# The opening of an mLSTM and MoE kernel in another order and smaller pieces, with its large tiles at multiples of 256 bytes

## The chip, the cores and the metric

The kernel runs on one core of one Trainium2 chip. The time is the device time of one execution in microseconds (us); lower is better. A core has five engines that run their own instruction streams and wait for each other by semaphores: TensorE (PE; its weight loads are listed as PEld), VectorE (DVE), ScalarE (ACT), GpSimd (POOL) and SyncE (SP), which here only issues transfers. Matmuls take their operands from SBUF and write PSUM, whose eight banks are handed out as tiles.

## The reference

Three stages, all in float32:

- An mLSTM over 2 sequences of 768 steps with 8 heads of 40: per step a running maximum m of the gates, a matrix memory C and a vector n with decay exp(f + m_old - m) and input weight exp(i - m), and the output y = sigmoid(o) * (C q) / max(|n q|, 1).
- A mixture of four experts on the 1536 tokens of 320 features: out = sum over e of p_e * relu(x w1[e]) w2[e], with 1024 hidden features and p the normalised domain_probs.
- A gated layer: ((x w_a) * (x w_b)) w_out, with 1536 hidden features.

## The kernel before

**Precision.** A float32 operand that goes through fast matmuls (type fp32r) is kept as a high part and the rest, `wh` and `wl` for weights, `xh` and `xl` for x, `hh` and `hl` for hidden values, and a product adds up three terms. High parts come from a cast, low parts from a subtraction.

**Weights.** There are 14 blocks (8 of the experts, 6 of the gated layer). A block of the experts is 2816 columns, loaded in eight pieces of 352 (`piece1`). It is a generator of three steps: issue the load of the raw piece; cast it to `wh` on ACT; subtract to `wl` on POOL or DVE, as the table LOENG says. Raw pieces of blocks 0 to 2 lie in the space of `acc`, the sums that are not yet in use; a piece whose place is still in use makes its load wait, and SP with it. Blocks lie in three places: pool `wp0` (0, 1, 2, 4, 5, 6, 9, 10, 11), `wp1` (3, 7, 12) and `wx` (8, 13). By the sizes of the tiles allocated ahead of them the tiles of `wp0`, x (`xp`) and h (`hp`, `hp2`) start 160 bytes over a multiple of 256, those of `wp1` 224 and those of `wx` 96; all offsets inside a tile are multiples of 256.

**Tokens.** They go in 12 tiles n of 128, two tiles (one of each sequence) to a chunk j. A tile passes: gates (`gate1`, `gate_d`, `gate2`, `gate_c`, then hi and low parts into `zh`, `zx` and `LT`, and `build_R`, which spreads L over the heads into `Rr`); decay weights (`mask_of`, `weights_of` on PE, `w_exp` on ACT, `w_mask` on POOL; only the chunks 0 and 1 do it this way); scores q k (`scores2` or `scores`, tile `pt_c`); their product `s1b` on DVE; `s2a` on PE (`pt_y`, and from chunk 1 on `pt_i` with the state); `s2b` and `s2x` on DVE, which give x (`x_t`); three transposes `s3a`, then `x_hi` on ACT and `x_lo` on DVE. The state of a sequence moves on by `weigh_k`, `state` (`pt_u`), `state_in`, `state_old`, `state_add`.

**Order.** Scheduling is manual: each engine runs its instructions in the order in which the program emits them. The list `ev` (from L701) holds pairs of a slot number and a call, is sorted by slot, and is emitted between the items of the first stage. An item k is one hidden block of 128 features for 256 tokens: a first product of eight matmuls (L209, into `psa`), its eviction by ACT (`hh`, L276) and DVE (`hl`, L277), and two items later the second product of six matmuls (L288 to L290). Slots under 0 come ahead of item 0; there are 12 items for each pair of tiles, so item 12 needs x of the tiles 2 and 3. Two tiles of `psa` and two of `psb` take turns, and four PSUM tiles `ps_t` serve the attention work. Matmuls of a dummy operand (`warm_up`, `pt_w`) fill gaps of PE.

**Later.** From block 3 on the weights meet 512 tokens at a time, in `quad_a` (L229: 60 matmuls of 512 columns, two at once in two halves of the rows; weights are the loaded operand, x streams) and `quad_b` (L254: h is loaded, weights stream).

What the change touches: `piece1` (L75 on) and its table of places; `warm_up` (L641 on); `mask_of` (L481 on); `s2x` (L562 on) with its third multiply L577; `s2c` (L626 on); the list from L701 to about slot 12; and the pools' sizes.

Of the kernel before, what the change touches and what calls it, by code (L numbers as in the profile page):

```python
# [33 lines left out]
LOENG = {0: "ppvppppp", 1: "pppvpppv", 2: "ppppvvvp", 3: "vpvpvpvp", 4: "vpvpvpvp", 5: "vpvpvpvp"}  # L34
# [15 lines left out]
def mlstm_moe_kernel(ctx, tc, gates, qk, qc, kvo, dp, w1b, w2b, ident_d, bdmask_d, rsel_d, exp_d, out):  # L50
# [24 lines left out]
    def piece1(i, s, pool, lo_eng, apart=False, dma=None):  # L75
# [231 lines left out]
    with ExitStack() as c1:  # L307
# [9 lines left out]
        G = 112  # L317
        bdmask = ac.tile([120, 3, 3 * DE], F32, name="bdmask")
# [243 lines left out]
        def s2x(n):  # L562
# [10 lines left out]
            if j == 0:  # L573
# [3 lines left out]
                nc.vector.tensor_tensor(x[:, DM:], xu.rearrange("p h d -> p (h d)")[:, 256:DM], og[j][:, b, 256:DM], op=ALU.mult)  # L577
# [48 lines left out]
        def s2c(n):  # L626
            x = td[n]["x"]
            nc.scalar.copy(x[:, DM:], x[:, 256:DM])
# [12 lines left out]
        def warm_up(n):  # L641

            for _ in range(n):
                nc.tensor.matmul(pw, wz[:, 0:P], wz, start=True, stop=True)
# [14 lines left out]
        w0, w1, w2 = ([piece1(i, f, wp0, nc.vector if LOENG[i][f] == "v" else nc.gpsimd) for f in range(NP1)] for i in range(3))  # L659
# [340 lines left out]
```

## Time and profile before

| what | us |
|---|---|
| median of 3 runs | 611.43 |
| lowest, highest | 611.16, 614.92 |
| the profiled execution | 613.7 |
| its span, first to last instruction | 612.0 |
| PE busy in the span | 599.4 |
| DVE, ACT, POOL busy | 406.4, 274.6, 189.3 |

The profile is of one execution. Its span leaves out what lies around the first and last instruction. Busy is the time in which an engine has at least one instruction running; since matmuls overlap, a PE that is busy all the time may still run them further apart than it could. PE's granted clock has two levels, 1.2 and 2.4 GHz; the profile gives the share of the full one.

### The profile page before, as it was taken

To read this page: it belongs to the slowest core of one execution; us is meant where nothing else is said; L and a number is where in the kernel's file an instruction comes from. 1 tells how busy PE (TensorE), PEld (TensorE's weight loads), DVE (VectorE), ACT (ScalarE), POOL (GpSimd) and SP (SyncE) were. 2 spreads that over 40 slices of the span, in tenths; PEclk is the share of its full clock that TensorE was granted. 3 is DMA by queue.
4 is the path that set the end of the run, shared out by engine and by line. 5 is a ranking of instruction groups with operands and counts; after the bars stand their busy time and mean duration, and the time that the engine had idled before them with its cause. 6 is when DMAs were issued, how large, how long until landed. Compare 5 with 4: busy or idle time off the path is not lost.

```text
span 612.0 us, 14366 instructions
## 1 busy us (share of the span) xinstructions
PE 599.4 (98%) x5815; PEld 564.3 (92%) x5816; DVE 406.4 (66%) x820; ACT 274.6 (45%) x633; POOL 189.3 (31%) x225
## 2 busy tenths in 40 slices
PE   8789999999999999999999999999999999999997
PEld 5689999999999899999999999988898989888886
DVE  6978767676553243323789899898777787864344
ACT  7737566666533323333344343454553434341211
POOL 2756516363511111334243333333222222310000
PEclk9989999999999999999999999999999999999999
DMA  8956473738202122322222222222121120200012
GB/s 246 251 172 168 134 203 90 212 81 221 59 13 69 36 60 74 82 73 76 57 76 59 72 71 60 57 64 65 47 49 45 37 56 22 69 4 2 2 44 87
DMA packets 29344, 51.51 MB, mean 84 GB/s; under 512 B 3509, under 2 KB 18141, under 8 KB 29277
## 3 DMA queue, kind: packets, MB, share of 16 engines
q1 hardware_dynamic: 15869, 26.06, 15.5%
q10 hardware_dynamic: 12496, 22.16, 13.4%
q0 software_dynamic: 912, 2.36, 1.3%
q8 instruction: 46, 0.75, 0.5%
q14 instruction: 21, 0.17, 0.1%
HBM read 47.79 MB, written 2.00 MB: 81 GB/s over the span
## 4 chain that ended last, share of the span: by engine, by line
PE 93%; DVE 4%; DMA 1%; issue 0%; ACT 0%; SPq 0%; DVEq 0%; ACTq 0%
PE psy L254 27%; PE psa L229 27%; PE psb L229 11%; PE psa L209 10%; PE psy L288 3%; PE pt_y L539 3%; PE psy L290 3%; PE psy L289 3%; PE pt_i L545 1%; PE pt_c L525 1%; PE pt_u L601 1%; DMA qk_t<-in_qk 1%; DVE Rr L478 1%; PE pt_x L146 0%; DVE qs_t L353 0%
## 5 line engine op out<-in xcount | busy, mean ns | idle before, releaser
L229 PE MATMUL psa<-xh,wh 64*128 64x512 f32 x576 | 135.2, 390 | 0.0
L254 PE MATMUL psy<-wl,hh 64*128 64x320 f32 x752 | 131.4, 305 | 0.0
L254 PE MATMUL psy<-wh,hh 64*128 64x320 f32 x752 | 131.3, 305 | 0.0
L254 PE MATMUL psy<-wh,hl 64*128 64x320 f32 x752 | 131.2, 305 | 0.0
L229 PE MATMUL psa<-xh,wl 64*128 64x512 f32 x414 | 97.4, 389 | 0.0
L254 PEld LDWEIGHTS psy<-wh,hh 64*128 64x128 f32 x752 | 85.7, 184 | 0.8
L229 PEld LDWEIGHTS psa<-xh,wh 64*128 64x128 f32 x576 | 80.9, 184 | 5.9 <-issue 0.9
L254 PEld LDWEIGHTS psy<-wl,hh 64*128 64x128 f32 x752 | 85.5, 184 | 0.8
L254 PEld LDWEIGHTS psy<-wh,hl 64*128 64x128 f32 x752 | 85.7, 184 | 0.0
L229 PE MATMUL psa<-xl,wh 64*128 64x512 f32 x384 | 85.6, 389 | 0.0
L849 DVE SCALAR_TENSOR_TENSOR hl<-psa,hh 128x512 fp32r<-128x512 f32 x60 | 38.6, 685 | 54.8 <-ACT hh L848 54.4
L126 POOL TENSOR_TENSOR wl<-tp,lf 128x272 fp32r<-128x272 f32 x48 | 39.1, 814 | 113.0 <-DVE tp L125 111.3
L229 PE MATMUL psb<-xh,wh 64*128 64x512 f32 x216 | 69.8, 389 | 0.0
L229 PEld LDWEIGHTS psa<-xh,wl 64*128 64x128 f32 x414 | 60.7, 184 | 3.7
L229 PE MATMUL psb<-xh,wl 64*128 64x512 f32 x180 | 58.5, 389 | 0.0
L229 PEld LDWEIGHTS psa<-xl,wh 64*128 64x128 f32 x384 | 55.2, 184 | 3.6
L277 DVE SCALAR_TENSOR_TENSOR hl<-psa,hh 128x256 fp32r<-128x256 f32 x72 | 30.4, 422 | 41.4 <-ACT hh L276 40.9
L123 POOL TENSOR_TENSOR lf<-lf,sq 128x272 f32<-128x272 f32 x48 | 38.1, 795 | 62.6 <-ACT wh L122 48.7
L94 POOL TENSOR_TENSOR wl<-raw,wh 128x352 fp32r<-128x352 f32 x28 | 26.4, 948 | 95.1 <-ACT wh L92 68.7
L276 ACT ACTIVATE hh<-psa 128x256 fp32r<-128x256 f32 x72 | 27.6, 384 | 60.5 <-PE psa L209 59.7
L848 ACT ACTIVATE hh<-psa 128x512 fp32r<-128x512 f32 x60 | 32.6, 596 | 46.7 <-PE psy L254 26.9
L209 PE MATMUL psa<-xh,wh 128*128 128x256 f32 x216 | 51.6, 293 | 1.3 <-DVE hl L277 1.0
(146 smaller groups left out, 1424.5 us busy)
## 6 DMA issues: line engine op xcount, KB each, us to landing
raw<-in_w2b ACTq DMA_DIRECT2D x48, 272.0 KB, 2.8
qk_t<-in_qk SPq DMA_DIRECT2D x16, 480.0 KB, 5.5
raw<-in_w1b ACTq DMA_DIRECT2D x32, 176.0 KB, 2.3
acc<-in_w1b SPq DMA_DIRECT2D x24, 176.0 KB, 3.9
kvo_t<-in_kvo SPq DMA_DIRECT2D x10, 364.5 KB, 5.9
Rr<-dL_t ACTq DMA_DIRECT2D x5, 512.0 KB, 4.5
og_t<-in_kvo SPq DMA_DIRECT2D x6, 320.0 KB, 5.0
out<-acc SPq DMA_DIRECT2D x12, 160.0 KB, 1.9
```

The source lines that it names most:

```text
L94: lo_eng.tensor_tensor(wl[:, cs], raw, wh[:, cs].bitcast(F32), op=ALU.subtract)
L123: nc.gpsimd.tensor_tensor(lf, lf, sq, op=ALU.mult)
L126: nc.gpsimd.tensor_tensor(wl[:, cs], tf, lf, op=ALU.add)
L209: nc.tensor.matmul(ps, l, r, start=(i == 0), stop=(i == len(prs) - 1))
L229: return nc.tensor.matmul(ps[g], w[rows, o:o + P], x, start=start, stop=stop)
L254: ms = [nc.tensor.matmul(ps[t], l[rows, t * P:(t + 1) * P], w[rows, off:off + DM], start=start, stop=stop) for t, rows in zip(two, (UP, DN))]
L276: nc.scalar.activation(self.hh, ps, AF.Relu)
L277: nc.vector.scalar_tensor_tensor(self.hl, ps, 0.0, self.hh.bitcast(F32), op0=ALU.max, op1=ALU.subtract)
L288: nc.tensor.matmul(ps, lh, wh[:, off:off + DM], start=(fi == 0), stop=False)
L289: nc.tensor.matmul(ps, lh, wl[:, off:off + DM], start=False, stop=False)
L848: nc.scalar.activation(hh, ps[f], AF.Relu)
L849: nc.vector.scalar_tensor_tensor(hl, ps[f], 0.0, hh.bitcast(F32), op0=ALU.max, op1=ALU.subtract)
```

## The change

- **Pieces.** The places of raw pieces come from a table LAND; the third and fourth piece of block 1 use the rotating raw tiles instead of places in `acc`. The casts of the first two pieces of block 0 move from ACT to POOL, and all of block 0's subtractions are on POOL (one was on DVE). Subtractions that POOL does for blocks 0 to 2 are split into two halves of 176 columns.
- **x.** In chunk 0 the third multiply (the 64 columns that are kept twice) is replaced by a copy on POOL (`s2c`); the copies of tiles 2 and 3 move from ACT to POOL.
- **First loads.** The gates and two of the four first q/k loads go from SP's queue to ACT's, the other two and `rsel` from ACT's to SP's. Later loads come in another order.
- **Opening.** The four masks come together, the scores of tile 1 behind the weights of tile 0; hi and low parts of the gates are made on DVE; the first chunk's `build_R` uses DVE and ACT, not POOL; there are fewer fillers.
- **Second chunk.** Gates, weights, scores, states and the pieces of blocks 1 and 2 get other slots between 0 and 12.
- **Addresses.** `dpt` and `psm` move into the space of the last `acc` tile; small tiles `even`, `side` and `brim` are added that nothing reads or writes. With them `wp0`, `wp1`, `wx`, x and h start at multiples of 256.

```diff
-LOENG = {0: "ppvppppp", 1: "pppvpppv", 2: "ppppvvvp", 3: "vpvpvpvp", 4: "vpvpvpvp", 5: "vpvpvpvp"}
+LOENG = {0: "pppppppp", 1: "pppvpppv", 2: "ppppvvvp", 3: "vpvpvpvp", 4: "vpvpvpvp", 5: "vpvpvpvp"}
+LAND = ((0, 1, 2, 3, 4, 5, 6, 7), (8, 9, None, None, 0, 1, 2, 3), (4, 5, 6, 7, 8, 9, 2, 3))
...
-    dpt = const.tile([P, NT, E], F32, name="dpt")
     pg = const.tile([P, NT, E], F32, name="pg")
-    psm = const.tile([P, NT, 1], F32, name="psm")
+    even = const.tile([P, 24], F32, name="even")
+    side = ctx.enter_context(tc.tile_pool(name="side", bufs=1, side="right")).tile([P, 56], F32, name="side")
...
-        if i < 3:
-            at = (s if i == 0 else 8 + s if s < 2 else s) * st
-            raw = sums[:, at:at + st]
+        at = LAND[i][s] if i < 3 else None
+        if at is not None:
+            raw = sums[:, at * st:(at + 1) * st]
...
-        nc.scalar.copy(wh[:, cs], raw)
+        copy_on(hi_eng, wh[:, cs], raw)
         yield
-        lo_eng.tensor_tensor(wl[:, cs], raw, wh[:, cs].bitcast(F32), op=ALU.subtract)
+        parts = 2 if i < 3 and lo_eng is nc.gpsimd else 1
+        for k in range(parts):
+            ps = slice(s * st + k * st // parts, s * st + (k + 1) * st // parts)
+            lo_eng.tensor_tensor(wl[:, ps], raw[:, k * st // parts:(k + 1) * st // parts], wh[:, ps].bitcast(F32), op=ALU.subtract)
...
-                nc.vector.tensor_tensor(x[:, DM:], xu.rearrange("p h d -> p (h d)")[:, 256:DM], og[j][:, b, 256:DM], op=ALU.mult)
...
-        def s2c(n):
+        def s2c(n, eng=nc.scalar):
             x = td[n]["x"]
-            nc.scalar.copy(x[:, DM:], x[:, 256:DM])
+            copy_on(eng, x[:, DM:], x[:, 256:DM])
...
-            (-40, load_gates, 0, nc.sync), (-39.9, load_rsel, nc.scalar), (-39.8, load_qk, 0, 0, nc.sync), (-39.7, load_qk, 0, 1, nc.scalar),
+            (-40, load_gates, 0, A_), (-39.9, load_rsel, nc.sync), (-39.8, load_qk, 0, 0, A_), (-39.7, load_qk, 0, 1, nc.sync),
...
-            (-35, mask_of, 0, 0, ps_b, "b"), (-34.95, mask_of, 0, 1, ps_b, "b"), (-34.93, mask_of, 1, 0, ps_a, "a"), (-34.9, scores2, 0), (-34.85, warm_up, 1), (-34.83, scores2, 1),
-            (-34.81, warm_up, 0), (-34.8, gate1, 0), (-34.7, gate_d, 0, V), (-34.5, gate2, 0), (-34.4, gate_c, 0), (-34.3, hi_L, 0, nc.scalar),
-            (-34.2, hi_cm, 0, nc.gpsimd), (-34.15, top_cm, 0, nc.scalar), (-34.1, low_L, 0), (-33.9, low_cm, 0, nc.gpsimd),
-            (-33.8, build_R, 0, V, 0, 4), (-33.7, build_R, 1, nc.gpsimd, 0, 4), (-33.6, build_R, 0, nc.scalar, 4, 8), (-33.5, build_R, 1, V, 4, 8),
-            (-33, weights_of, 0, 0), (-32.9, w_exp, 0, 0), (-32.7, weights_of, 0, 1),
+            (-35, mask_of, 0, 0, ps_b, "b"), (-34.95, mask_of, 0, 1, ps_b, "b"), (-34.93, mask_of, 1, 0, ps_a, "a"), (-34.92, mask_of, 1, 1),
+            (-34.9, scores2, 0),
+            (-34.8, gate1, 0), (-34.7, gate_d, 0, V), (-34.5, gate2, 0), (-34.4, hi_L, 0, V), (-34.3, low_L, 0),
+            (-34.2, build_R, 0, V, 0, 4), (-34.15, gate_c, 0), (-34.1, hi_cm, 0, V), (-34.05, low_cm, 0), (-34, build_R, 0, A_, 4, 8),
+            (-33.9, build_R, 1, V, 0, 4), (-33.8, build_R, 1, A_, 4, 8),
+            (-33, weights_of, 0, 0), (-32.9, w_exp, 0, 0), (-32.7, weights_of, 0, 1), (-32.6, w_exp, 0, 1),
+            (-32.5, scores2, 1), (-32.4, weights_of, 1, 0), (-32.3, w_exp, 1, 0), (-32.1, weights_of, 1, 1), (-32, w_exp, 1, 1),
...
-            (-28.9, go, w0[4:5]), (-28.88, go, w0[5:6]), (-28.87, gate1, 1), (-28.86, gate_d, 1, V), ...
+            ... (-28.5, gate1, 1), (0.2, gate_d, 1, V), (0.3, gate2, 1), ...
...
-            ... (3.871, weights_of, 2, 0), ... (5.343, scores2, 3), ... (5.45, state, 1), ... (5.523, load_kvo, 3), ...
-            ... (5.6, s2a, 2, 1), ... (5.9, weights_of, 3, 0), ... (7.379, s2a, 3, 0), ...
+            ... (2.3, build_R, 2, V, 0, 4), ... (3.25, build_R, 2, V, 4, 8), ... (4.7, weights_of, 2, 0), ... (5.74, load_kvo, 3),
+            ... (5.8, weights_of, 3, 0), ... (6.5, weights, ), ... (6.7, scores2, 3), ... (6.88, send_L, 2, nc.sync), ... (6.91, state, 0), ...
+            ... (7.1, s2a, 2, 1), ... (7.45, spread_L, 4, nc.sync), ... (7.6, s2a, 3, 0), ... (8.12, state, 1), ...
...
+    brim = ctx.enter_context(tc.tile_pool(name="brim", bufs=1, reuse_waits="tile")).tile([P, 16], F32, name="brim")
```

## Rows read from the trace of the kernel before

**Rows 1.** The profile page: busy us by engine (share of the span, instructions).
```profile
PE 599.4 (98%) x5815; PEld 564.3 (92%) x5816; DVE 406.4 (66%) x820; ACT 274.6 (45%) x633; POOL 189.3 (31%) x225
```

**Rows 2.** Stretches: busy us (x instructions) of PE, PEld, DVE, ACT, POOL; clock; DMA share, GB/s.
```profile
18.90:59.00 40.10, 35.33 (x256) 33.01 (x257) 33.69 (x66) 25.88 (x62) 27.09 (x28) 0.96 0.69 193
59.00:75.00 16.00, 15.24 (x123) 15.01 (x123) 12.39 (x25) 10.35 (x30) 7.64 (x11) 1.00 0.43 112
...
25.00:30.00 5.00, 3.70 (x23) 2.86 (x23) 4.87 (x8) 4.74 (x14) 3.90 (x6) 1.00 0.68 201
30.00:35.00 5.00, 4.17 (x38) 3.74 (x37) 4.97 (x8) 3.06 (x9) 5.00 (x6) 1.00 0.42 109
35.00:40.00 5.00, 4.26 (x23) 4.19 (x22) 3.27 (x8) 0.48 (x1) 1.03 (x1) 0.66 0.36 102
```

**Rows 3.** Opening by time: start, length, engine, line; in brackets the wait before.
```profile
7.98 1.16 PE L517 MATMUL pt_c<-qk_t 40*128 40x128 f32 x16
...
9.07 0.98 PE L494 MATMUL pt_a<-Rr,LT 112*128 112x512 f32 x3
...
14.32 3.01 POOL L94 TENSOR_TENSOR wl<-acc,wh 128x352 fp32r<-128x352 f32 x3 [5.90 <-DMA qk_t<-in_qk]
14.68 0.96 DVE L577 TENSOR_TENSOR x_t<-xu_t,og_t 128x64 f32<-128x64 f32 x1
...
17.61 0.21 DVE L577 TENSOR_TENSOR x_t<-xu_t,og_t 128x64 f32<-128x64 f32 x1
...
18.92 0.50 PE L209 MATMUL psa<-xh,wh 128*128 128x256 f32 x2 [0.35 <-ACT xh L134]
```

**Rows 4.** Chain of the first items and just after: start, length, what.
```profile
52.79 0.63 PE pt_u L601 x6
...
59.14 0.96 PE psa L209 x8
...
71.55 0.85 PE pt_y L539 x8
72.41 0.70 PE pt_i L545 x6
```

**Rows 5.** PE's waits from 0 to 75 us: total, times, longest.
```profile
PE psa L209 <- DVE hl L277: 1.0, 2, 0.8
PE pt_a L494 <- DVE Rr L478: 0.9, 1, 0.9
PE pt_c L517 <- DVE w_t L529: 0.8, 1, 0.8
...
PE pt_u L601 <- DVE cbd_t L609: 0.7, 1, 0.7
```

**Rows 6.** DVE, POOL and ACT by time, columns as in rows 3.
```profile
4.60 0.29 DVE L393 TENSOR_TENSOR df<-fa,gt 112x128 f32<-112x128 f32 x1
...
6.62 2.35 DVE L478 TENSOR_TENSOR Rr<-zx,rsel 64x512 fp32r<-64x512 f32 x2
...
19.33 3.81 POOL L94 TENSOR_TENSOR wl<-acc,wh 128x352 fp32r<-128x352 f32 x4 [1.99 <-ACT wh L92]
...
20.59 0.86 DVE L393 TENSOR_TENSOR df<-fa,gt 112x128 f32<-112x128 f32 x1
...
44.87 0.24 ACT L628 COPY x_t<-x_t 128x64 f32<-128x64 f32 x1
```

**Rows 7.** Chain of the row-paired stage: start, length, what.
```profile
311.02 6.83 PE psa L229 x60
...
366.46 7.00 PE psa L229 x60
...
579.84 3.51 PE psy L254 x48
...
590.24 3.52 PE psy L254 x48
```

**Rows 8.** DMA issues of the first 40 us: KB each, median us to landing.
```profile
kvo_t<-in_kvo SPq DMA_DIRECT2D x3, 364.5 KB, 6.5
```

More of the change, by code (lines that the diff above doesn't have):

```diff
@@ L73, in mlstm_moe_kernel, with copy_on, piece1 @@
     wblk = {}
-    def piece1(i, s, pool, lo_eng, apart=False, dma=None):
+    def copy_on(eng, o, i):
+        (eng.copy if eng is nc.scalar else eng.tensor_copy)(o, i)
+    def piece1(i, s, pool, lo_eng, apart=False, dma=None, hi_eng=nc.scalar):
         if s == 0:
@@ L317, in mlstm_moe_kernel @@
         G = 112
+        dpt = sums[:, 3776:3824].rearrange("p (n e) -> p n e", e=E)
+        psm = sums[:, 3824:3836].unsqueeze(2)
         bdmask = ac.tile([120, 3, 3 * DE], F32, name="bdmask")
@@ L639, in mlstm_moe_kernel, with warm_up @@
         nc.gpsimd.memset(wz, 0.0)
-        def warm_up(n):
+        def warm_up(n, ps=None):
+            if ps is None:
+                ps = ps_b.tile([P, 512], F32, tag="b", name="pt_w")
             for _ in range(n):
-                nc.tensor.matmul(pw, wz[:, 0:P], wz, start=True, stop=True)
+                nc.tensor.matmul(ps, wz[:, 0:P], wz, start=True, stop=True)
         def go(gens):
@@ L657, in weights @@
             nc.vector.tensor_tensor(pg, dpt, psm.to_broadcast([P, NT, E]), op=ALU.mult)
-        w0, w1, w2 = ([piece1(i, f, wp0, nc.vector if LOENG[i][f] == "v" else nc.gpsimd) for f in range(NP1)] for i in range(3))
+        w0, w1, w2 = ([piece1(i, f, wp0, nc.vector if LOENG[i][f] == "v" else nc.gpsimd, hi_eng=nc.gpsimd if i == 0 and f < 2 else nc.scalar) for f in range(NP1)] for i in range(3))
         V = nc.vector
@@ new lines, in mlstm_moe_kernel @@
+            (1.5, go, w1[1:2]), (2.2, go, w1[2:3]), (2.21, go, w1[3:4]), (2.25, hi_cm, 1, V), (2.26, low_cm, 1), (2.3, build_R, 2, V, 0, 4),
+            (2.4, go, w1[2:3]), (3.1, go, w1[3:4]), (3.15, go, w1[4:5]), (3.2, go, w1[5:6]), (3.25, build_R, 2, V, 4, 8),
+            (3.3, gate4, 0), (3.31, gate5, 0), (3.4, go, w1[4:5]), (3.6, build_R, 3, V, 0, 4), (4.1, go, w1[6:7]), (4.15, go, w1[7:8]),
+            (4.4, gate_tail, 0), (4.45, gate_out, 0),
+            (4.7, weights_of, 2, 0), (4.71, w_exp, 2, 0), (4.72, w_mask, 2, 0), (4.73, go, w1[5:6]), (4.8, build_R, 3, V, 4, 8), (4.9, s1b, 2, 0),
@@ new lines, in mlstm_moe_kernel @@
+            (5.1, gate4, 1), (5.11, gate5, 1),
+            (5.3, weights_of, 2, 1), (5.31, w_exp, 2, 1), (5.32, w_mask, 2, 1), (5.4, go, w1[6:7]), (5.5, s1b, 2, 1), (5.6, go, w1[7:8]),
+            (5.7, go, w2[4:5]), (5.71, go, w2[5:6]), (5.72, go, w2[6:7]), (5.73, go, w2[7:8]), (5.74, load_kvo, 3),
+            (5.8, weights_of, 3, 0), (5.81, w_exp, 3, 0), (5.82, w_mask, 3, 0), (5.85, weigh_k, 0),
+            (6.1, go, w2[0:1]), (6.2, go, w2[1:2]), (6.3, s2a, 2, 0),
+            (6.5, weights, ), (6.52, gate1, 2), (6.53, gate_d, 2, V), (6.55, weights_of, 3, 1), (6.56, w_exp, 3, 1), (6.57, w_mask, 3, 1), (6.6, gate_tail, 1), (6.62, gate_out, 1), (6.64, table, AF.Sigmoid), (6.65, o_gate, 2),
@@ new lines, in mlstm_moe_kernel @@
+            (6.7, scores2, 3), (6.75, go, w2[0:1]), (6.8, go, w2[1:2]), (6.85, s1b, 3, 0), (6.87, gate2, 2), (6.88, send_L, 2, nc.sync), (6.94, gate_c, 2),
+            (6.9, state_old, 0), (6.91, state, 0), (6.92, state_in, 0), (6.93, state_add, 0), (7.1, s2a, 2, 1), (7.15, go, w2[2:3]), (7.16, go, w2[3:4]), (7.18, table, AF.Exp), (7.2, s2b, 2), (7.25, s2x, 2), (7.3, s2c, 2, P_), (7.35, s1b, 3, 1),
+            (6.98, weigh_k, 1), (7.45, spread_L, 4, nc.sync), (7.55, spread_L, 5, nc.sync), (7.4, go, w2[2:3]), (7.5, go, w2[3:4]), (7.6, s2a, 3, 0),
@@ new lines, in mlstm_moe_kernel @@
+            (8.1, state_old, 1), (8.12, state, 1), (8.13, state_in, 1), (8.14, state_add, 1), (8.15, go, w2[4:5]), (8.16, go, w2[5:6]),
+            (8.2, s3a, 2), (8.25, x_hi, 2), (8.3, x_lo, 2), (8.4, go, w2[4:5]), (8.45, go, w2[5:6]), (8.5, s2a, 3, 1), (8.6, s2b, 3), (8.65, s2x, 3), (8.7, s2c, 3, P_),
+             (7.95, weigh_k, 2), (8.8, go, w2[6:7]), (8.9, go, w2[6:7]),
+            (9.1, go, w2[7:8]), (9.3, go, w2[7:8]),
+            (9.65, weigh_k, 3),
+            (8.0, load_qk, 4, 0), (8.02, load_kvo, 4), (9.75, load_gates, 3), (8.03, load_qk, 4, 1),
```

71 lines of the change are left out of this document (27 added, 44 removed).

## The prediction

> **What bounds it now.** I read the page's busy times, then the stretches, then the opening in order of time, then the chain and TensorE's waits. TensorE (PE) is busy for 98% of the span [rows 1], so time can only come from three places: the opening before the first product of the experts, the waits behind it, and the length of a matmul itself. The stretches place the waits: from 59 to 75 us PE is busy for 15.2 of 16.0, before that it is idle or slow again and again [rows 2]. The first product starts at 18.92, released by the cast of xh [rows 3]; the thirteenth item, near which the touched order ends, starts at about 59.0 (59.14 where the chain cuts it) [rows 4]. That stretch is 40.1 us. PE's work in it, from rows where it runs without a wait [rows 3, 4]: 12 first products at 0.96 (11.5), 10 second products of six matmuls at 0.147 (8.8; a pair of the same 320 columns takes 3.51/24 in [rows 7]), four s2a at 0.85 (3.4), two pt_i at 0.70 (1.4), four states at 0.63 (2.5), one scores2 at 1.16 and four weight matmuls of 0.3 or less (2.2), and 1.0 for the transposes, an estimate from their columns. That is 30.8, so 9.3 us are lost there. Of them 3.4 are the four longest waits [rows 5] and 1.7 the clock: 0.66 of it granted over the 5 us from 35 on, so partly the lower level of 1.2 GHz, after the waits of 0.8 and 0.7 [rows 2, 5]. The rest is short waits and the refill of PE after each. In the same stretch VectorE (DVE) is busy for 33.7 of 40.1, and at 97% (4.87 of 5) from 25 to 30 [rows 2]: it is DVE that PE waits for.
>
> **Term a, up to the first product.** Now the scores of the second tile start at 7.98, the weight matmuls behind them at 9.07, x of the second tile is done at 17.82 (17.61 and 0.21) [rows 3]. The new order puts the weight matmuls of tile 0 ahead of the scores of tile 1. They then wait for the gates, since low_cm goes from GpSimd (POOL) to DVE, behind the first build_R. The first of two builds begins at 6.62, 2.35 for both [rows 6]; with cm moved behind it, it begins near 6.35 and ends near 7.5, and three small instructions of about 0.3 (the subtract's 0.29 [rows 6]) make LT ready near 8.5, some 0.5 before 9.07. From there PE is bound by the 32 pt_y matmuls, which wait for the same DVE products as now; I take 0.25 of the 0.5. On x, the third multiply of each tile goes: 0.96, about 0.9 of it behind the one before, and 0.21 [rows 3]. In its place stands a copy of 64 columns on POOL. ScalarE (ACT) does that copy in 0.24 [rows 6]; for POOL no row has it, and I take 0.4 for the one that counts, the second (0.24 below, 0.95 above, where a piece of wl stands ahead of it). 0.25 + 1.1 - 0.4 is about 0.9; the wl piece that ran on DVE leaves the queue ahead of the low part of x, for which I add 0.3. **a = 1.2**, between 0 and 2.0. Costed at nothing: the casts of the first two pieces of w0 go from ACT to POOL, which stood idle for 5.9 us up to 14.32 [rows 3] and has done them before x. The first loads trade places between SP and ACT, three issues on each ahead of the scores as before; ACT's table load starts some 0.3 later and is covered by the wait for zx, and without that cover the 0.3 would be paid once.
>
> **Term b, from the first product to the thirteenth.** What each wait is now and what the change does to it [rows 5, 6]. The 0.8 for hl: DVE does the scan and the subtract of the second pair (the latter 0.86) ahead of the first eviction; the subtract moves behind it. The 0.9 for Rr: weights_of(2) goes from slot 3.87 to 4.7, its builds end a slot before. The 0.8 of scores2(3), for a bank that s1b must free, moves from slot 5.3 to 6.7, and the 0.7 of the state products from 5.45 to 8.12. Loads: w1's first pieces get places of their own, so SP waits less for pieces of w0 to be used up, with qk, kvo and gates behind it; the spread of L goes from ACT to SP. Against that, DVE's own work stays: it adds hi_L (about 0.3) and moves nothing off after the first product. So DVE sets the bound: 33.7 us at the 97% that it has reached are 34.7, and 0.7 I leave for evictions that it cannot begin before PE's product ends: 35.4 against 40.1. **b = 4.6** with the hi_L. The ends are 0 (DVE idles as often as now) and 9.3 (its instructions shrink beside shorter ones of POOL, and PE never waits). Late next: POOL makes the low pieces of w0 at 0.95 each (3.81 for four [rows 6]) behind the second copy of x, so that items 2 and 3 may wait some 0.3 each, and in slots 3 and 8 DVE has four to six long instructions ahead of an eviction. Both are within what is left of the 9.3.
>
> The subtract took 0.86 beside POOL's pieces and 0.29 ahead of them [rows 6]. The Trainium skill, SBUF — State Buffer, section "SBUF: two separate sides", says that VectorE with two SBUF inputs and GpSimd take a port pair in turn, and that the first holds it for its whole instruction; the trace agrees with these 0.86. By that rule pieces of half the length would shorten a block by 0.24 on average, at some ten meetings 2.4 us (an estimate from that page), and the sum would be 10.0 in place of 7.6; by the same rule the copies that POOL takes over from ACT block DVE, which speaks against the change. The sum takes neither; shorter instructions on DVE are priced from rows as a rival below.
>
> **Term c, the addresses.** The sizes of the tiles put wp0 (blocks 0 to 2, 4 to 6, 9 to 11), x and h at 160 bytes over a multiple of 256, wp1 (3, 7, 12) at 224 and wx (8, 13) at 96. The row-paired stage differs in step with that: the 60 matmuls of quad_a take 6.83 with wp0 and 7.00 with wp1, and with wx a second product of 3.51 begins 10.40 before the next, which leaves 6.89 [rows 7]. The second products keep their 3.5 with wx and, by the chain, elsewhere, and in them the weights stream and h is loaded; so it is the loaded operand that matters. If multiples of 256 run like wp0, the nine units of wp1 save 0.17 each (1.5) and the six of wx 0.06 or less (0.3). **c = 1.8.** No row has these tiles at 0. The other end is that 0 is as bad as 224: the 24 quads that are not in wp1 pay 0.17 (4.1), and the 576 first products' matmuls of the 72 items the same 5.8 ns (3.3), together 7.4. More gain than 2.0 is left out: 6.83/30 is 14 ns over 512 columns at 2.4 GHz and 3.51/24 is 13 ns over 320, alike for two sizes and two places, so that rest looks like a fixed step. I take 1.8, since wp0 is the level of most rows and the distance from weights to x, 0 in wp0, is 0 everywhere afterwards.
>
> The 550 us behind the thirteenth item are otherwise not touched; dpt and psm, now in the space of the last acc tile, are read at slot 6.5, long before that tile is written.
>
> **Sum.** 1.2 + 4.6 + 1.8 = 7.6. The profiled execution took 613.7 (612.0 of span and 1.7 around it); one like it would take 606.1. It stands 2.3 over the median of the runs, 611.43, from which the forecast is 603.8, said as 604.
>
> **Rivals.** *The waits only change place.* load_kvo(3) is issued at slot 5.74, but its buffer is that of tile 0, free when state(0) has run at 6.91, and s2a(3) needs it at 7.6. Between them PE has a first and a second product, half an s2a with pt_i: about 3.4 us. A kvo load took 6.5 from issue to landing in the first 40 us [rows 8]: PE would wait some 3 us, and the clock could fall as at 35 us (1.7). Behind the waiting load SP holds send_L(2), both spreads of L and the loads of tile 4, all for slot 12 and later. For it: on PE state(0) stands behind scores2(3) and weights_of(3), which need banks that DVE and ACT free; against: the DMA share was 0.42 after 30 us and 0.68 before [rows 2]. 603.8 + 4.6 is 608.4, which is also b = 0. 22 in 100. *The addresses have nothing to do with it*, the 0.17 belongs to what runs beside: c = 0, 605.6. 12 in 100. *Full closing*: b near 8, as DVE's instructions get short without POOL's long pieces: 600.4. 16 in 100. *The clock falls in the opening*: the single fillers between scores, weights and pt_y go, and PE waits about 1 us before the weights. After waits of 0.8 and 0.7 the clock fell once [rows 2, 5]; at its lower level the 32 pt_y would take 4 times 0.85, 3.4 us, more [rows 4]: 607.2. 8 in 100. The Trainium skill, TensorE: Matmul & The Clock Gate, section "HAM oscillation — how this bites in real kernels", warns of idle stretches between bursts of matmuls; the trace agrees at 35 us. *Slower*: multiples of 256 cost what 224 costs, in every quad and item: 7.4 against a gain of 5.8 from a and b, 613.0. It decides from 7.00 per quad on. For it stands only that nothing lies there now, against it wp0. 7 in 100.
>
> **Numbers.** The forecast itself, 601 to 606.5, has 35 in 100. A measurement of this kernel can tell about 1%, 6.1 us: faster is under 605.3, slower over 617.5. Faster: 0.25 of the forecast's own, 0.16 of full closing, 0.09 of the address case and the others: 0.50. Slower: 0.05, the slower rival with less than a and b gained. Same: 0.45. The range goes from full closing with c and a at their best to the moved waits with half of a: 598 to 610.
>
> **What would show it.** The first product near 17.7; the thirteenth item 35 to 36 us later; PE's waits for hl, Rr and cbd gone and the clock at 1.00 from 35 to 40; quads of blocks 3, 7 and 12 at 6.83. Wrong if a wait for kvo_t or a low clock stands before 45 us, if DVE's work in the stretch grows, or if quads with wp0 leave 6.83.

## The result, and the profile after

| | before | after |
|---|---|---|
| median, us (4 runs each) | 611.90 | 605.81 |
| lowest to highest | 611.16 to 614.92 | 605.27 to 606.00 |
| the profiled execution | 613.7 | 606.0 |
| its span | 612.0 | 604.3 |

The 611.90 has one run more than the 611.43 from which the forecast was taken. The ratio is 0.989, with an interval from 0.9855 to 0.9924: 6 us less. The forecast of 604.0 was 1.8 too low. A first account comes from four stretches of the two traces:

| stretch | before | after | difference | predicted |
|---|---|---|---|---|
| first product of item 0 starts | 18.92 | 17.19 | -1.7 | -1.2 (a) |
| from there to the thirteenth item | 40.05 | 35.48 | -4.6 | -4.6 (b) |
| from there to the row-paired stage | 145.14 | 145.51 | +0.4 | 0 |
| first quad_a to the start of the last second product of a block | 396.37 | 394.49 | -1.9 | -1.8 (c) |
| sum | | | -7.8 | -7.6 |

The profiled executions differ by 7.7 us, just as the sum said, yet the medians differ by 6.1. Where the other 1.6 us went is answered behind the experiments, in the first point on the prediction.

The page after, busy times, against [rows 1]: PE has lost 5.6 us of busy time while its number of instructions stayed (two fewer on the page). So part of the gain is work that got shorter, not waits that went.

```profile
PE 593.8 (98%) x5813; PEld 561.1 (93%) x5814; DVE 403.5 (67%) x821; ACT 273.3 (45%) x630; POOL 193.0 (32%) x248
```

The stretches after (columns as in [rows 2]; line numbers of the changed kernel are 5 to 9 higher from here on):

```profile
17.20:52.70 35.50, 33.33 (x256) 31.42 (x257) 31.35 (x68) 25.45 (x59) 27.68 (x45) 1.00 0.82 232
...
25.00:30.00 5.00, 4.93 (x35) 4.52 (x33) 4.73 (x9) 3.93 (x10) 5.00 (x7) 1.00 1.08 292
30.00:35.00 5.00, 4.90 (x44) 4.37 (x43) 4.50 (x10) 3.88 (x9) 5.00 (x9) 1.00 0.39 126
35.00:40.00 5.00, 3.82 (x32) 3.67 (x32) 4.34 (x11) 2.62 (x5) 1.62 (x3) 1.00 0.46 141
```

PE's busy share from the first product to the thirteenth item rises from 88% to 94%, the clock from 35 to 40 is 1.00 where it was 0.66, and DVE's work is 31.35 us, not 33.69. The largest hole left lies in the 5 us from 35 on; a second, of 0.6, stands at 47.9. PE's waits from 0 to 75 us (total, times, longest), against [rows 5], say which ones:

```profile
...
PE pt_i L551 <- DVE cbd_t L614: 1.2, 1, 1.2
PE pt_a L500 <- DVE LT L443: 1.2, 1, 1.2
PE pt_c L531 <- DVE qs_t L362: 0.9, 1, 0.9
PE pt_x L153 <- DVE x_t L585: 0.6, 1, 0.6
PE psa L216 <- ACT xh L141: 0.4, 1, 0.4
...
```

All four long waits of [rows 5] behind the first product are gone: hl, Rr, the bank of w_t, and cbd ahead of pt_u. A new one for cbd, longer than the old (1.18 against 0.7), stands elsewhere, ahead of pt_i at 37.4. The opening by time, against [rows 3] and [rows 6]:

```profile
6.41 0.68 DVE L484 TENSOR_TENSOR Rr<-zx,rsel 64x512 fp32r<-64x512 f32 x1
...
8.19 0.70 PE L500 MATMUL pt_a<-Rr,LT 112*128 112x512 f32 x2 [1.16 <-DVE LT L443]
...
8.82 1.16 PE L523 MATMUL pt_c<-qk_t 40*128 40x128 f32 x16
...
15.94 0.24 POOL L77 COPY x_t<-x_t 128x64 f32<-128x64 f32 x1 [0.41 <-DVE x_t L582]
...
17.19 0.51 PE L216 MATMUL psa<-xh,wh 128*128 128x256 f32 x2 [0.35 <-ACT xh L141]
...
19.28 0.29 DVE L402 TENSOR_TENSOR df<-fa,gt 112x128 f32<-112x128 f32 x1
```

The first weights start at 8.19 (9.07 before), after a wait for LT; the scores of tile 1 come behind them. One build_R took 0.68 where two took 2.35 beside POOL's [rows 6], the copy on POOL 0.24, and the subtract of the second pair 0.29 in place of 0.86.

The chain of work from 20 to 38 us in the changed kernel (start, length, what), to be set beside the sentence "it is DVE that PE waits for":

```profile
22.80 4.41 POOL wl L101 x6
27.21 1.05 POOL w_t L513
28.25 1.49 POOL wl L101 x2
29.74 0.60 POOL w_t L513
...
30.36 0.69 DVE w_t L535
...
36.02 0.80 issue
36.82 0.52 DVE cbd_t L614
...
37.39 0.93 PE pt_i L551 x6
```

The end of the hole at 37.39 is followed back over DVE to 30.36 and from there over 7.5 us of POOL; PE's own products are not on this chain. The row-paired stage, against [rows 7]: the block that had quads of 7.00 has 6.83, and the half blocks of wx follow one another in 10.34, where it was 10.40.

```profile
318.42 6.83 PE psa L236 x60
...
360.00 6.83 PE psa L236 x60
...
572.15 3.52 PE psy L261 x48
...
582.49 3.52 PE psy L261 x48
```

### The profile page after: what moved, and what is told of

The parts are those of the page before. It is cut to its first block, busy times and chain, and to the rows that moved or that the text cites. A ratio compares the mean times of both kernels' runs of the same rounds, so it can differ in the third digit from the quotient of the medians.

```text
span 604.3 us, 14381 instructions
## 1 busy us (share of the span) xinstructions
PE 593.8 (98%) x5813; PEld 561.1 (93%) x5814; DVE 403.5 (67%) x821; ACT 273.3 (45%) x630; POOL 193.0 (32%) x248
## 4 chain that ended last, share of the span: by engine, by line
PE 93%; DVE 3%; POOL 1%; ACT 1%; DMA 1%; issue 0%; DVEq 0%
PE psy L261 27%; PE psa L236 27%; PE psb L236 11%; PE psa L216 10%; PE psy L295 3%; PE psy L297 3%; PE psy L296 3%; PE pt_y L545 3%; PE pt_i L551 1%; PE pt_c L531 1%; POOL wl L101 1%; PE pt_u L606 1%; DVE qs_t L362 1%; DMA gt<-in_gates 1%; PE pt_x L153 1%
## 5 line engine op out<-in xcount | busy, mean ns | idle before, releaser
L261 PE MATMUL psy<-wh,hl 64*128 64x320 f32 x752 | 139.9, 306 | 0.0
L261 PE MATMUL psy<-wh,hh 64*128 64x320 f32 x752 | 139.8, 306 | 0.0
L261 PE MATMUL psy<-wl,hh 64*128 64x320 f32 x752 | 139.8, 306 | 0.0
L236 PE MATMUL psa<-xh,wh 64*128 64x512 f32 x576 | 137.2, 389 | 0.0
L261 PEld LDWEIGHTS psy<-wl,hh 64*128 64x128 f32 x752 | 94.0, 184 | 0.8
L261 PEld LDWEIGHTS psy<-wh,hh 64*128 64x128 f32 x752 | 94.0, 184 | 0.7
L261 PEld LDWEIGHTS psy<-wh,hl 64*128 64x128 f32 x752 | 94.1, 184 | 0.0
L236 PEld LDWEIGHTS psa<-xh,wh 64*128 64x128 f32 x576 | 84.5, 184 | 5.7 <-issue 0.9
L236 PEld LDWEIGHTS psa<-xh,wl 64*128 64x128 f32 x414 | 62.7, 184 | 3.6
L101 POOL TENSOR_TENSOR wl<-raw,wh 128x352 fp32r<-128x352 f32 (+1 forms) x30 | 28.1, 940 | 94.5 <-ACT wh L77 68.1
```

Source lines behind the costliest of these rows:

```text
L101: lo_eng.tensor_tensor(wl[:, ps], raw[:, k * st // parts:(k + 1) * st // parts], wh[:, ps].bitcast(F32), op=ALU.subtract)
L236: return nc.tensor.matmul(ps[g], w[rows, o:o + P], x, start=start, stop=stop)
L261: ms = [nc.tensor.matmul(ps[t], l[rows, t * P:(t + 1) * P], w[rows, off:off + DM], start=start, stop=stop) for t, rows in zip(two, (UP, DN))]
```

## The experiments

"Stage" below is the time from the first quad_a to the start of the last second product of a block: 396.37 before, 394.49 after. In the comparison of the first four experiments the kernel before has a median of 611.34 (31 executions); each of the four has ten.

**1. Only the addresses.** The kernel before with the moved `dpt` and `psm` and the three unused tiles, its own order left.

```diff
-    dpt = const.tile([P, NT, E], F32, name="dpt")
-    psm = const.tile([P, NT, 1], F32, name="psm")
+    even = const.tile([P, 24], F32, name="even")
+    side = ctx.enter_context(tc.tile_pool(name="side", bufs=1, side="right")).tile([P, 56], F32, name="side")
...
+        dpt = sums[:, 3776:3824].rearrange("p (n e) -> p n e", e=E)
+        psm = sums[:, 3824:3836].unsqueeze(2)
...
+    brim = ctx.enter_context(tc.tile_pool(name="brim", bufs=1, reuse_waits="tile")).tile([P, 16], F32, name="brim")
```

> The kernel before with the address edits alone. If the address of the loaded weights sets the length of a quad: the quads of blocks 3, 7, 12 and 13 fall to 6.83 us, the row-paired stage shortens by 1.9 us, the opening (first product 18.9, thirteenth item 40.1 later) stays, and the time falls by 1.9 (ratio 0.997). If the quads of wp1 and wx were slow for what runs beside them: 7.00 and 6.89 stay and the time is that of before.

Measured: 610.20 us, ratio 0.9979 [0.9949, 1.0009]; stage 394.48, 1.89 shorter. By the times alone this is no difference; the trace decides, since the stage is PE's own work and repeats to 0.02 us. The chain of the stage (start, length, what):

```profile
362.71 6.83 PE psa L229 x60
...
585.20 3.52 PE psy L254 x48
...
595.54 3.52 PE psy L254 x48
```

The block at 362 has 6.83 and the half blocks 10.34, with the old order around them. So c belongs to the addresses. The opening did not stay as expected: the first product starts at 18.49 and the thirteenth item 37.25 later, with the clock at 1.00 and less work on DVE (columns as in [rows 2]).

```profile
18.50:55.70 37.20, 33.68 (x255) 31.41 (x256) 32.34 (x66) 25.26 (x62) 27.55 (x28) 1.00 0.73 207
```

This trace is of the fastest of the ten executions (608.76).

**2. The new order at the old addresses.** The three unused tiles out, `even` at 64 columns, so that wp0, x and h lie at 160, wp1 at 224, wx at 96 again.

```diff
-    even = const.tile([P, 24], F32, name="even")
-    side = ctx.enter_context(tc.tile_pool(name="side", bufs=1, side="right")).tile([P, 56], F32, name="side")
+    even = const.tile([P, 64], F32, name="even")
...
-    brim = ctx.enter_context(tc.tile_pool(name="brim", bufs=1, reuse_waits="tile")).tile([P, 16], F32, name="brim")
```

> The changed kernel with wp0, x and h back at 160 over a multiple of 256, wp1 at 224, wx at 96. By the address theory: quads of blocks 3, 7 and 12 at 7.00, of 13 at 6.89, time 1.9 over the changed kernel, about 607.7; the opening as in the changed kernel (first product 17.2, thirteenth item at 52.7). If addresses also matter to the opening's engines, the thirteenth item moves by 0.5 us or more.

Measured: 607.94 us, ratio 0.9937 [0.9909, 0.9965]; stage 396.37, the figure of before to the hundredth; first product 17.31 and 35.44 to the thirteenth item, as after, so the opening does not depend on the addresses. The chain of the stage:

```profile
361.73 7.00 PE psa L235 x60
...
585.50 3.52 PE psy L260 x48
...
595.90 3.52 PE psy L260 x48
```

7.00 and 10.40 are back. The two parts of the change don't touch each other, apart from a second wait for qs_t, of 1.2 us at 63 us, that no other of these traces has. By the medians the order is worth 3.4 us (between 2.1 and 5.6 by the interval), not the 5.8 of a + b.

**3. Whole pieces.** POOL's subtractions not halved.

```diff
-        parts = 2 if i < 3 and lo_eng is nc.gpsimd else 1
+        parts = 1
```

> The changed kernel with POOL's subtractions whole again (352 columns, not two of 176). If shorter blocks of the port are what relieves DVE: DVE's busy time from the first product to the thirteenth item goes from 31.4 back towards 33.7, and the stretch grows by 1 to 2.4 us. If the order alone did it: the stretch stays within 0.5 of 35.5, time within 0.5 of 605.8.

Measured: 606.54 us, ratio 0.9919 [0.9889, 0.995]; first product 17.26. The stretch from there to the thirteenth item (columns as in [rows 2]):

```profile
17.26:53.10 35.84, 33.64 (x255) 31.25 (x256) 32.17 (x68) 25.32 (x59) 24.05 (x29) 1.00 0.77 220
```

With whole pieces DVE does 0.8 us more in the same number of instructions, PE waits 0.9 for hl again, and the row-paired stage starts 0.35 later. The scan of the second pair's gates, same place in the order, in number 3 and then in the changed kernel, and PE's wait in number 3:

```profile
18.02 1.18 DVE L398 TENSOR_TENSOR_SCAN fa<-gt,fa 112x128 f32<-112x128 f32 x1
```

```profile
17.95 0.58 DVE L398 TENSOR_TENSOR_SCAN fa<-gt,fa 112x128 f32<-112x128 f32 x1
```

```profile
PE psa L216 <- DVE hl L284: 0.9, 2, 0.6
```

So the halves shorten what DVE does beside POOL, but the wait for cbd shrinks from 1.18 to 0.61 at the same time, and by the trace only 0.35 reaches the row-paired stage. The medians cannot tell: the interval, 604.6 to 608.3 us, holds the 605.81 of the changed kernel. One of the ten executions took 611.76, at a mean clock of 0.986.

**4. The old slots.** The changed kernel with the second chunk's gates, weights, scores, products, x and states (72 calls) at the slots of the kernel before.

```diff
+        EARLY = {('gate1', 1): -28.87, ('gate_d', 1): -28.86, ('gate2', 1): 0.6, ...
+        ev = [(EARLY.get((e[1].__name__,) + tuple(x for x in e[2:] if isinstance(x, int)), e[0]),) + e[1:] for e in ev]
```

> The changed kernel with the second chunk's attention work (72 calls) at the slots of the kernel before; pieces, loads, opening and addresses stay changed. If the later slots are what took PE's waits away: the waits for hl, Rr, w_t and cbd come back and the thirteenth item moves from 52.7 to 55 or later, time 608 or more. If the relief of DVE (opening, short pieces, loads) did it: the thirteenth item stays within 1 us of 52.7.

Measured: 608.46 us, ratio 0.9943 [0.9915, 0.9972]; 39.0 us to the thirteenth item, row-paired stage 2.5 later than after. PE's waits from 0 to 75 us, and the stretch from 45 to 50:

```profile
PE pt_y L545 <- DVE w_t L535: 2.0, 1, 2.0
...
PE pt_u L606 <- POOL kw_t L594: 1.3, 1, 1.3
PE pt_a L500 <- DVE LT L443: 0.8, 1, 0.8
PE pt_a L500 <- DVE y_t L561: 0.6, 1, 0.6
```

```profile
45.00:50.00 5.00, 5.00 (x29) 5.00 (x30) 4.37 (x12) 0.89 (x3) 2.10 (x3) 0.66 0.84 261
```

The old slots cost 2.5 us at the row-paired stage and bring the low clock back: a wait of 2.0 is followed by PE at 0.66 over 5 us, as in [rows 2], and nine of the ten executions have a mean clock of 0.997 or less. The expectation named four waits that should return. Of them only 0.2 for Rr did; hl, cbd and the bank of w_t did not. The waits that stand there now, for w_t ahead of pt_y and for kw_t, are others.

**5 to 7. Three more sets of addresses.** Each moves tiles of the changed kernel by 64 bytes through other sizes of the unused tiles; in the third `pg` moves too.

```diff
# 5: weights, x and h all 64 above a multiple of 256
-    even = const.tile([P, 24], F32, name="even")
-    side = ...tile([P, 56], F32, name="side")
+    even = const.tile([P, 40], F32, name="even")
+    side = ...tile([P, 40], F32, name="side")
# 6: weights at a multiple, x and h 64 above
+    gap = xp.tile([P, 16], F32, name="gap")
...
-    brim = ...tile([P, 16], F32, name="brim")
# 7: weights 64 above, x and h at a multiple
-    pg = const.tile([P, NT, E], F32, name="pg")
...
-    side = ...tile([P, 56], F32, name="side")
+    side = ...tile([P, 40], F32, name="side")
+    pg = xp.tile([P, NT, E], F32, name="pg")
...
-    brim = ...tile([P, 16], F32, name="brim")
+    brim = ...tile([P, 32], F32, name="brim")
```

> Weights, x and h all lie 64 bytes above a multiple of 256, as far from one another as in the changed kernel. If only the distance of the weights from x counts: all row-paired quads after the first two at 6825 ns, the stage at 394.5 us. If the place itself (a multiple of 256) counts: quads near 7000 ns (224 against 160 in the kernel before) or 6885, the stage 1.8 to 5 us longer.

> Weights at multiples of 256 as in the changed kernel, x and h 64 bytes above one, so the weights lie 64 below x (as wx did in the kernel before). Distance theory: all quads after the first two near 6885 ns, 28 x 0.06 = 1.7 us on the stage (396.2 us). Theory that only the weights' own place counts: 6825, 394.5 us. Theory that every buffer has to be at a multiple of 256: near 7000, 399.4 us.

> Weights 64 bytes above a multiple of 256, x and h at one, so the weights lie 64 above x (as wp1 did in the kernel before). Distance theory: all quads after the first two near 7000 ns, 28 x 0.175 = 4.9 us on the stage (399.4 us). Theory that only x's own place counts: 6825, 394.5 us. Theory that a distance of 64 on either side costs the same: the same as with x 64 above.

Measured, one execution each:

| | weights minus x | quads after the first two | stage | execution |
|---|---|---|---|---|
| changed kernel | 0 | 6.825 | 394.49 | 606.0 |
| 5 | 0 | 6.825 | 394.50 | 605.72 |
| 6 | -64 | 6.87 and 6.89 | 396.40 | 606.46 |
| 7 | +64 | 7.00 | 400.29 | 610.81 |

Rows of the chain (start, length, what), of the changed kernel, of 6 and of 7: a first product of one of the last items, and for 6 and 7 quads of 60 matmuls, in 7 with a second product of 96 ahead of one:

```profile
189.05 0.96 PE psa L216 x8
```

```profile
186.67 0.94 PE psa L217 x8
...
318.37 6.89 PE psa L237 x60
...
332.30 6.87 PE psa L237 x60
```

```profile
189.02 0.93 PE psa L216 x8
...
312.76 7.04 PE psy L261 x96
319.80 7.00 PE psa L236 x60
```

The distance decides, not the place: all at 64 runs like all at 0. Only the distances 0, 64 and -64 were tried. The distance also gives the levels of the kernel before, where wp1 lay 64 above x (7.00) and wx 64 below (6.89).

**8. The third multiply back.** In chunk 0 the multiply of 64 columns on DVE in place of the copy on POOL.

```diff
+                nc.vector.tensor_tensor(x[:, DM:], xu.rearrange("p h d -> p (h d)")[:, 256:DM], og[j][:, b, 256:DM], op=ALU.mult)
...
-            ... (-30.05, s2c, 0, P_), ... (-29.6, s2c, 1, P_), ...
```

> The changed kernel with the third 64-wide multiply on VectorE back for items 0 and 1 in place of the copy on GpSimd. If the dropped multiply is what brings the first product forward: VectorE does 0.2 to 0.3 us more, once for item 0 and once for item 1, and the first product starts 0.2 to 0.4 us later, at 17.4 to 17.6 us. If the earlier first product comes from the scores, masks and the splitting of build_R alone: 17.2, unchanged.

Measured: one execution of 605.70; first product 17.92, 0.73 later, more than expected. But the ninth item starts at 39.83 (39.85 in the changed kernel), and the row-paired stage at 198.19 (198.18). PE in order of time:

```profile
17.92 0.47 PE L216 MATMUL psa<-xh,wh 128*128 128x256 f32 x2 [0.23 <-POOL wl L101]
...
37.37 0.93 PE L551 MATMUL pt_i<-cbd_t,qc_t 120*128 120x123 f32 x6 [1.00 <-DVE cbd_t L615]
```

The later start is made up for before the ninth item: the seventh starts 0.40 later than in the changed kernel, the eighth 0.15, and the wait for cbd at 37.4 is 1.00 in place of 1.18. The chain over POOL and DVE ends that wait at the same time either way. The multiply is worth 0.7 at the first product and nothing at the end.

**9 and 10. Against the waits that are left.** Both put pair 2's gates behind `state_in` of item 0, and the scores of item 4's second half behind more of PE's work; 9 gives one build_R of the opening to POOL besides, 10 moves the gates further back.

```diff
# both
-            (13.285, scores, 4, 1), ...
+            (14.3, scores, 4, 1), ...
# 9
-            (-34.2, build_R, 0, V, 0, 4), ...
+            (-34.2, build_R, 0, P_, 0, 4), ...
-            ... (6.87, gate2, 2), (6.88, send_L, 2, nc.sync), (6.94, gate_c, 2),
+            ... (6.935, gate2, 2), (6.936, send_L, 2, nc.sync), (6.94, gate_c, 2),
# 10
+            ... (7.27, gate2, 2), (7.28, send_L, 2, nc.sync), (7.29, gate_c, 2),
```

> The changed kernel with three waits attacked. gate2 and send_L of pair 2 moved from 6.87 to 6.935, behind state_in of item 0 (6.92): VectorE then makes cbd 1.4 us earlier, and if VectorE's order is what PE waits for there, the wait for cbd (1.18 us at 37.4) goes and items from the 9th on start 1.0 to 1.2 us earlier; if VectorE's sum of work is the limit, the wait turns up again within three items (hl, y_t or x_t). scores of item 4's second half at 14.3 in place of 13.285: the wait for qs_t (0.85 us at 56.9) goes, or turns into one for hl. build_R of item 0 on GpSimd in place of VectorE: first weights 0.3 to 0.5 us earlier, first product near 16.8; if VectorE's work up to 37 us sets the 9th item, as the kernel with the third multiply showed, nothing of that reaches it. Together 603.5 to 604.9 us.

> As the kernel before this one for pair 2's gates and for scores of item 4, but gate2, send_L and gate_c of pair 2 at 7.27 to 7.29, behind the normalisation of item 2 too, and the opening as in the changed kernel. If VectorE's order counts: the wait for cbd goes as with 6.935, and the wait for x_t (0.62 us at 47.9) goes too or stays. If the gates become late for pair 2: a wait for LT, Rr or w_t between 54 and 60 us, of 1 us or more. 603.5 to 606 us.

Measured, one execution each: 603.97 and 604.26. In both the wait for cbd is gone; the ninth item starts 0.9 and 1.3 earlier than in the changed kernel, the seventeenth 1.3 and 1.0. In 10 PE waits 0.9 for w_t at 41.6 in its place. build_R on POOL brought the first product to 17.47, later than in the changed kernel and not at 16.8: that expectation was wrong.

**11 and 12. The better version and the changed kernel side by side.** 11 is number 9 without the edit of build_R; 12 is the changed kernel as it is.

> The changed kernel with gate2 and send_L of pair 2 at 6.935 and scores of item 4's second half at 14.3, the opening left as it is. If both waits stay away as in the kernel with build_R on GpSimd: first product at 17.2, the row-paired stage from 196.6 us (198.2 in the changed kernel), 603.5 to 604.3 us in the median, 1.5 to 2 us below the changed kernel. If typical executions of the changed kernel don't have the waits that its profile shows: no difference.

> The changed kernel itself, for a comparison on the same chip: 605.3 to 606.2 us in the median; granted clock 1.0 in nearly every execution, while the kernel before has some executions with a lower one.

Measured, same chip: 604.32 us (603.82 to 605.39; ratio to before 0.9865 [0.9837, 0.9893]) and 605.81 us (605.44 to 606.67; 0.9887 [0.9857, 0.9918]). All six executions of 11 lie below all six of 12: 1.5 us by the medians. Number 11 is 1.3% below the kernel before and 0.25% below the changed one. The opening and the row-paired stage came later than expected, at 17.49 and 197.30 (17.2 and 196.6). DVE and PE of 11 in order of time:

```profile
35.74 0.53 DVE L614 TENSOR_TENSOR cbd_t<-pt_u,bdmask 120x369 f32<-120x369 f32 x1
36.19 0.81 DVE L406 TENSOR_SCALAR lf<-df 112x128 f32<-112x128 f32 x1
37.03 0.42 DVE L408 TENSOR_TENSOR_SCAN L<-rmask,lf 112x128 f32<-112x128 f32 x1
```

```profile
36.33 0.93 PE L551 MATMUL pt_i<-cbd_t,qc_t 120*128 120x123 f32 x6
```

cbd comes 1.1 earlier because two instructions of the gates now stand behind it, and pt_i follows without a wait. The ninth item starts 1.0 earlier than in the changed kernel, the thirteenth 0.4 and the row-paired stage 0.9.

## Why the prediction was right, point by point

**The sum and what it was taken from: the step that failed.** The prediction took 7.6 off the median, 611.43, though the sum was worked out in an execution of 613.7. It noticed the 2.3 between them and went on as if they were a part that the change leaves alone. They are not. For an execution like the profiled one it said 606.1, and the profiled execution of the changed kernel took 606.0; the step from there to the median is what failed. The profiled execution before had PE at half clock for 3.4 us:

```profile
36.20:39.60 3.40, 3.40 (x17) 3.40 (x16) 2.08 (x5) 0.00 (x0) 0.00 (x0) 0.50 0.42 109
```

That is the kernel before from 36.2 to 39.6, about 1.7 us lost (half of 3.4, PE being busy throughout), and most executions of it don't have this. Of its 43 executions beside the experiments, 11 had a mean clock of 0.997 or less and took 611.6 to 618.2 us; the other 32 took 610.0 to 612.7, 611.1 in the median. (The profiled one had 0.997.) Of ten executions of the changed kernel with a clock on record none was below 0.999.

Number 1 shows the same from inside: the old order without a stretch of low clock, 18.49 to the first product and 37.25 from there to the thirteenth item, 3.2 earlier in sum than in the profiled execution before. So a + b is 6.3 in the profiled pair, but 3.1 against number 1's trace, which is of a fast execution, 3.4 by the medians of number 2, and 4.4 by the median of number 1 against 605.81, two kernels that did not run side by side. With the 1.9 of c that makes 5.0 to 6.3. The medians of the kernel before, 611.34 to 612.34 in three comparisons, lie 5.5 to 6.5 above the 605.81 that the changed kernel has in both of its comparisons. The executions of the kernel before without a low clock have a median only 5.3 above it; that the rest comes from those with a low clock fits the counts but was not shown.

Carried to the median, b should have been 4.6 less the 2.3 by which its execution stood above it, 1.7 of it the clock: 2.3. The sum would have been 5.3 and the forecast 606.1, an estimate that puts the whole 2.3 into b.

**Term a.** Sized too small, 1.2 against 1.7, and it counts for less than its size. LT was ready 0.3 earlier than expected (the weights start at 8.19, 0.9 ahead of 9.07 and not 0.5), the copy on POOL took 0.24 and not 0.4. That what starts earlier also ends earlier was assumed; number 8 shows that 0.73 of it is given back by the ninth item. Terms that share a later wait can't be added one by one; a + b was right as one term, and b would have come out smaller with a later start.

**Term b.** 35.48 against 35.4, but the argument behind it held in part only, and that the number agrees is luck: two errors cancel. DVE was to keep its 33.7 us and work at 97%. It did 31.35 in 35.5, which is 88%: less work, worse filled. Of the 2.3 less, 1.35 is also the distance between two traces of the old order (33.69, and 32.34 in number 1); POOL's halves account for 0.8 (number 3). And what PE waits for is not DVE's sum of work but a chain that runs over POOL's pieces and masks up to 30.3 and over DVE after it. That the order of DVE's queue stood behind the hole at 37.4 is shown by number 11, where the same 31.3 us of DVE work fit into 34.8.

The waits named in the prediction went, but not each for the reason given. For hl it was to be the subtract's move behind the first eviction. In number 4 the subtract stands ahead of it again and PE has no wait for hl; in number 3 it stands behind and PE waits 0.9. So it is the halves that took this wait away, by shorter instructions of DVE. For the other three number 4 gives no such proof: with the old slots they stay away too, but for 0.2 of Rr, and the time is lost in other waits and at the low clock.

On the port rule: the trace before gave 0.86 and 0.29 for the same subtract; in the new place it took 0.29 beside POOL's halves and 0.51 beside whole pieces (number 3), and the scan ahead of it 0.58 and 1.18. The Trainium skill, SBUF — State Buffer, section "SBUF: two separate sides", says that an instruction of VectorE with two inputs in SBUF and one of GpSimd that reads SBUF exclude each other for a whole instruction. The estimate from it was 2.4 us for the halves; number 3 measures 0.8 in DVE's busy time and 0.35 at the row-paired stage: the direction agrees, the size doesn't.

**Term c.** 1.88 against 1.8, and of the two reasons given the second was right. That the loaded operand alone matters fails on number 6, where the weights stay and only x and h move: 6.87 to 6.89 in place of 6.825. Number 5 excludes that multiples of 256 are special; the distance from weights to x, named in the prediction as the ground for taking 1.8, is what counts. The slower rival would have been half right at a distance of +64: the stage of number 7 is 3.9 longer than before, where 4.1 was reckoned, but the 3.3 that it reckoned for the first products has the other sign (last section).

**The rivals.** load_kvo(3): PE has no wait for kvo_t, and number 4's 608.5 shows what waits in other places cost. Addresses irrelevant: excluded by numbers 1 and 2. Full closing: no, PE is idle for 2.2 us of the stretch, though DVE's instructions did get shorter. The clock did not fall after the wait of 1.16 ahead of the weights, nor after the 1.18 at 37.4; after 2.0 in number 4 it did. But in the kernel before it fell after 0.8 and 0.7, so the length of one wait does not settle it. Of the observations listed for the forecast, 35.5, the clock at 1.00 and 6.83 came as said; the first product came at 17.19, not 17.7, and the waits for hl and Rr are gone while one for cbd stands at a new place.

**What stays open.** It is open why some executions of the kernel before have the low clock and others don't: only one execution of it has a trace, and that one has it. The second wait for qs_t in number 2 was not explained. Why DVE's work in the old order is 33.69 us in one trace and 32.34 in another is open too, and so is what made Rr, cbd and the bank of w_t ready in time with the old slots.

## What to carry to other kernels

Before a sum from a trace is taken off a median, ask what sets that execution apart, and above all whether a stall or a low clock that the sum removes is in most executions at all; an execution that stands 2.3 us over the median has told something. Terms that end at one common wait are one term: look for the next wait at which both come together, and price them there. When PE works without a gap and groups of the same matmuls have different lengths, compare where the operands lie.

## What the runs showed of the hardware that was not expected

- The spacing of matmuls depends on the distance between the two operands in SBUF, by the three distances tried modulo 256: 60 matmuls of a quad take 6.825 us at 0, 6.87 to 6.89 at -64 and 7.00 at +64 (weights minus x). The second products, where h is loaded and weights stream, stay at 7.04 for 96 matmuls. What in the chip makes it so was not shown.
- In the first products of the first stage, 256 columns and all 128 rows, the effect has the other sign: the eight matmuls of an item take 0.96 us at 0 (before and after alike), 0.94 at -64 and 0.93 at +64, the rows above. Over the 60 items from the thirteenth on that would be 1.0 to 1.5 us, an estimate from these rows before rounding. The stretch from there to the row-paired stage was in fact shorter by 0.8 (144.74, number 6) and 0.4 (145.11, number 7) than the 145.51 of the changed kernel, so part of it is lost in waits. Weights of the first three blocks 64 away from x, and the others at 0, was not tried.
- The clock is no fixed property of a program: 11 of 43 executions of the kernel before had a mean of 0.997 or less, one stretch of 3.4 us at half clock making up such a mean, and the others had next to none. The order shifts how often it happens: 9 of 10 with the old slots (number 4), none of 10 in the changed kernel.
